# Rest tokens' second scores inside M's step, batch 0 by halves of its heads, and a new order, in a two-stage attention with an MLP on one core

## The chip, the cores and the metric

The kernel runs on one core of a Trainium2 chip. The metric is device time in microseconds for one execution. The core has five engines with queues of their own: TensorE (PE: matmuls; PEld is its weight load), VectorE (DVE), ScalarE (ACT), GpSimd (POOL, which here issues the loads) and SyncE (SP, which here issues the stores). An engine works its queue strictly in order; an instruction that waits for another engine holds up everything behind it in its own queue. Matmul results go to PSUM, eight banks of 128 partitions by 512 float32 numbers, from which VectorE or ScalarE read them.

## The reference

For each of 8 batches and 8 heads, with 576 tokens of 64 numbers, a pack of 32 queries `p` first attends over the tokens; then the 576 queries `q` attend over the 32 packed rows; the heads side by side go through an MLP with a squared relu:

```python
p_packed = sm_attn(p, k, v)          # 32 x 64 per head
out = sm_attn(q, p_packed, p_packed) # 576 x 64 per head
x = out, heads side by side          # 4608 x 512
h = relu(x @ w_in); y = (h * h) @ w_out   # 512 -> 2048 -> 512
```

`sm_attn` is softmax attention with scale 1/8 and the row's maximum taken off. Inputs and output are float32; the kernel multiplies in bfloat16.

## The kernel before, in words

Heads are handled in two groups of four (`qd` 0 and 1). For one batch the steps are, with their names in the planner and their lines:

- **T** (Tk, Tq; L440, L437): VectorE transposes of k and q after the loads.
- **S1** (L449/L451 in `s1`, L464 in `s1_both`): first scores, 32 pack rows for four heads by 576 tokens per group. `s1` makes one group with 128x128 matmuls; `s1_both` makes both groups with 64x32 tiles of the array that work side by side. Batch 0 (`SOLO`) uses `s1`, the others `s1_both`. Then max (L472), exponential with its sum (L476) and normalisation (L482, L483).
- **E** (L489): five 128x128 transposes per group into one PSUM bank, 4 or 5, and a copy to SBUF (`s1_out`).
- **PV, XT** (L504, L516): the packed rows; `extract` copies them out of the bank as `ppT`, `spread` reorders them with four small matmuls into the same bank, and `pq_block` writes them as blocks on a diagonal into `pq_bd` (four copies).
- **M** (L536): packed rows times w_in, 64x32 tiles, in four chunks of 512 columns; so the second attention's value product and w_in become one matrix. Chunks are copied out by `m_out` (two banks at once) or `m_half` (one bank).
- **S2** (L556, L567 in batch 0): second scores, tokens on partitions, 512 of the 576 tokens. **S2 rest** (L574, `s2_rest`): the last 64 tokens, four matmuls with 128x64 tiles into bank 4 or 5. Then max (L586), subtract (L591), exponential (L597), sum and reciprocal (L603, L604), product (L609).
- **N** (L618, L620): transposes of these weights into bank 4 or 5, N.b.0 for the first 256 tokens, N.b.1 for the rest, and copies to `a2`.
- **F1** (L633; L646 in batch 0, called FA and F1): M times weights, 16 blocks of 128 rows, into a pair of banks; relu (L655, L671) and square (L662, L664, L681) give `gT`.
- **F2** (L689, and L706 for the last tile): 16 matmuls of 512 columns for each tile of 128 tokens, into bank 6 or 7 (two early tiles in banks 5 and 3), a copy (`f2_out`) and four stores.

Banks are named by tiles. `ps` holds two pair tiles, banks 0 and 1 and banks 2 and 3, each `[128, 2, 512]`; banks 4 to 7 are four tiles of one bank each, `pb4` to `pb7`. `bank(u)` gives one bank, `pair(u)` a pair tile. The framework adds the waits between engines from the tiles that the instructions read and write.

The order is written out ahead of time by a planner (`Plan`). It holds streams of steps, each with its dependencies, its PSUM banks and set durations (the number beside an engine's name), and issues what is ready by a priority. `TABLE` corrects priorities ("o") and the choice between VectorE and ScalarE ("l"). Where the planner sees TensorE idle before the first F2, it fills in matmuls on zeros (`keep_clock`, L345). POOL issues the loads; the string `ORDER` names them, and among the early ones `TABLE` decides which goes first.

Of the kernel before, what the change touches and what calls it, by code (L numbers as in the profile page):

```python
# [53 lines left out]
class Plan:  # L54
# [193 lines left out]
TABLE = {'o': {'P.0': -301.77, 'X.0': -1069.94, 'P.2': -238.95, 'X.1': -188.5, 'La0': -1231.77, 'La1': -809.34,  # L248
# [45 lines left out]


def kernel_impl(tc, q, k, v, p, w_in, w_out, out):
# [10 lines left out]
    NT = TOK // P  # L307
    NKQ, NV, NR = 15, 5, 6
    VX = JT // 2
    SOLO = (0,)  # L310
    TOKH = (2 * P, S - 2 * P)

    with ExitStack() as ctx:
# [23 lines left out]
        pq_bd = [consts.tile([P, 4 * P], BF16, name=f"pq_bd{i}") for i in range(2)]  # L337
# [9 lines left out]
        def half(n):  # L347
            return ps[n // 2][:, n % 2, :] if n < 4 else ps[n - 2][:]
# [14 lines left out]
        def setup():  # L363
            nc.vector.memset(zero, 0.0)  # L364
            nc.vector.memset(pT_bd[:, :2], 0.0)
            nc.vector.memset(v_b[0][:64, :, GM * D:], 0.0)
            nc.vector.memset(pq_bd[0], 0.0)
            nc.vector.memset(pq_bd[1], 0.0)
# [55 lines left out]
        class Att:  # L424
            def __init__(self, b, t):
                self.b, self.t = b, t
                self.pq = pq_bd[b % 2]
                self.ps1, self.psm, self.pst = {}, {}, {}
# [38 lines left out]
            def at(self, qd, h):  # L467
                return h ^ 2 if qd and self.b not in SOLO else h

# [25 lines left out]
            def pv(self, qd, u):  # L495
                if qd == 0:
                    self.ps_bank = bank(u)
                    self.ps_pp = self.ps_bank[:, :P]
# [20 lines left out]
            def pq_block(self, h, eng):  # L519
                c = slice(32 * h, 32 * h + 32)  # L520
                cast(eng, self.pq[c].rearrange("p (qd x c) -> p x qd c", qd=NQD, x=2)[:, :, :, c],
                     self.ps_pq[c].rearrange("p (x qd i) -> p x qd i", x=2, qd=NQD))

            def pq_of(self, qd, dh):
                return self.pq[:, (2 * qd + dh) * P:(2 * qd + dh + 1) * P]
# [33 lines left out]
            def s2_half(self, x, u):  # L559
                if x == 0:  # L560
                    self.ps2h = {}
# [7 lines left out]

            def s2_rest(self, u):  # L570
                self.ps2r = bank(u)[:, :P]
                for dh in range(2):
# [4 lines left out]
            def src2(self, x):  # L577
                s = self.ps2r if x == 2 else self.ps2h[x] if x < 2 else self.ps2[:].rearrange("p c n -> p (c n)")
                return s.rearrange("p (g i) -> p g i", i=32)
# [453 lines left out]
```

## Time and profile before

| | |
|---|---|
| median of three runs | 256.63 us (256.39 to 256.83) |
| profiled execution | 256.86 us, span 255.1 us |
| granted TensorE clock | 0.999 |
| TensorE busy | 246.8 us, 97% |
| VectorE, ScalarE busy | 172.9 us (68%), 168.3 us (66%) |
| F2 (L689) | 560 matmuls of 512 columns, 380 ns from start to end each, overlapping |
| F1 (L633) | 448 matmuls of 288 columns, 286 ns each, overlapping |

Matmuls overlap, so the pace is read from the distance of their starts in the timeline and not from their mean duration. The time of the profiled execution is 1.8 us above its span, which begins with the first instruction and ends with the last. Before 30 us batch 0 works through its chain, with filling matmuls between; from there TensorE goes through F1, F2 and the next batches' steps mixed. In a profile line, what stands in brackets is the idle time of the engine before the instruction and what ended it.

### The profile page before, as it was taken

Reading aid. Unit: us, or ns where it says so; the run is one execution under the profiler, and the core shown is the slowest. Engines: PE = TensorE matmul, PEld = TensorE weight load, DVE = VectorE, ACT = ScalarE, POOL = GpSimd, SP = SyncE. Lnnn points to the kernel's source line nnn. Section 1 sums busy time; section 2 is a strip of 40 time slices with the busy share of each in tenths; the row PEclk is TensorE's granted clock in tenths of the full one; section 3 lists DMA queues with packets and bytes.
Section 4 is the critical chain, followed back from the end, with each engine's and each line's share of the span. In section 5 each row is a group of like instructions: output and inputs, shape, how many; then the busy total and the mean of one; then the engine's idle time right before and its main releaser. Section 6 shows DMA issues by size and latency. Waiting matters only on the chain.

```text
span 255.1 us, 5879 instructions
## 1 busy us (share of the span) xinstructions
PE 246.8 (97%) x2348; PEld 139.9 (55%) x2348; DVE 172.9 (68%) x339; ACT 168.3 (66%) x289; POOL 43.0 (17%) x76
## 2 busy tenths in 40 slices
PE   7898999999999999999999999999999999999993
PEld 5574665365545665466454555467454565365452
DVE  6678767896886797576369369967768667546300
ACT  7436999779629488688676791599461685669301
POOL 8746444332424300000000000000000000000000
PEclk9999999999999999999999999999999999999999
DMA  6999999999999999510112202211111211111132
GB/s 113 189 201 208 202 204 201 214 245 230 205 224 226 237 219 159 129 45 0 44 44 62 63 3 70 56 41 42 38 51 41 54 31 36 49 51 31 48 93 68
DMA packets 26619, 28.50 MB, mean 112 GB/s; under 512 B 5472, under 2 KB 18016, under 8 KB 26592
## 3 DMA queue, kind: packets, MB, share of 16 engines
q0 software_dynamic: 18960, 18.55, 44.4%
q1 hardware_dynamic: 7008, 9.38, 13.4%
q8 instruction: 18, 0.29, 0.4%
q10 hardware_dynamic: 624, 0.20, 0.3%
q14 instruction: 9, 0.07, 0.1%
HBM read 37.22 MB, written 9.44 MB: 183 GB/s over the span
## 4 chain that ended last, share of the span: by engine, by line
PE 87%; ACT 4%; DMA 3%; DVE 2%; POOL 1%; issue 1%; DVEq 0%; POOLq 0%
PE pb L689 46%; PE ps L633 22%; DMA q_b<-in_q_dram 3%; PE ps L556 3%; PE pb L504 2%; PE ps L536 2%; PE ps L464 2%; PE ps L646 2%; PE pb L489 2%; PE pb L618 1%; PE ps L689 1%; PE pb L706 1%; PE pb L536 1%; ACT r L655 1%; ACT gT L662 1%; ACT pq_bd L359 1%
## 5 line engine op out<-in xcount | busy, mean ns | idle before, releaser
L689 PE MATMUL pb<-w_out_b,gT 128*128 128x512 bf16 x544 | 142.9, 380 | 0.0
L689 PEld LDWEIGHTS <-gT 128*128 128x128 bf16 x560 | 51.5, 97 | 56.2 <-issue 5.0
L671 ACT ACTIVATE r<-ps 128x576 bf16<-128x576 f32 x112 | 71.9, 651 | 15.7 <-PE ps L633 11.2
L633 PE MATMUL ps<-a,M 128*128 128x288 bf16 x448 | 72.2, 286 | 0.0
L681 DVE TENSOR_TENSOR gT<-r 128x576 bf16<-128x576 bf16 x112 | 50.6, 457 | 28.8 <-ACT r L671 27.8
L633 PEld LDWEIGHTS <-M 128*128 128x128 bf16 x448 | 43.2, 98 | 21.1 <-issue 1.3
L476 ACT ACTIVATE e1x<-ps,n 128x576 bf16<-128x576 f32 x16 | 11.8, 748 | 13.8 <-DVE n L472 13.0
L359 ACT CAST M<-ps 128x1024 bf16<-128x1024 f32 (+1 forms) x18 | 16.5, 916 | 6.0 <-PE ps L536 5.9
L361 DVE COPY o_sb<-pb 128x512 f32<-128x512 f32 (+1 forms) x20 | 13.2, 662 | 8.5 <-PE pb L706 4.5
L359 ACT COPY o_sb<-pb 128x512 f32<-128x512 f32 (+1 forms) x16 | 9.3, 579 | 14.0 <-PE pb L689 12.8
L597 ACT ACTIVATE e<-d 128x1152 bf16<-128x1152 f32 (+2 forms) x10 | 9.6, 970 | 12.8 <-DVE d L591 12.7
L472 DVE TENSOR_REDUCE n<-ps 128x1 f32<-128x576 f32 x16 | 11.6, 749 | 7.3 <-PE ps L464 7.1
L345 PE MATMUL pb<-zero 128*128 128x256 bf16 x92 | 14.3, 305 | 1.5 <-DVE zero L364 1.1
L359 ACT CAST M<-pb 128x512 bf16<-128x512 f32 x28 | 15.3, 601 | 0.0
L414 POOL DMA_DIRECT2D v_b<-in_v_dram x16 | 11.2, 702 | 13.3 <-DMA k_b<-in_k_dram 9.9
L437 DVE STREAM_TRANSPOSE qT<-q_b 128x576 f32<-128x576 f32 x16 | 11.8, 758 | 1.9 <-DMA q_b<-in_q_dram 1.9
L359 ACT COPY a<-pb 128x512 bf16<-128x512 bf16 (+1 forms) x9 | 5.4, 634 | 11.5 <-PE pb L618 10.9
L409 POOL DMA_DIRECT2D q_b<-in_q_dram x16 | 8.9, 560 | 22.6 <-DVE kT L440 10.5
L603 DVE TENSOR_REDUCE t<-e 128x36 f32<-128x1152 bf16 (+2 forms) x10 | 11.1, 1105 | 2.1 <-ACT e L597 2.0
L440 DVE STREAM_TRANSPOSE kT<-k_b 128x576 f32<-128x576 f32 x16 | 11.9, 762 | 0.8 <-DMA k_b<-in_k_dram 0.8
L345 PEld LDWEIGHTS <-zero 128*128 128x128 bf16 x92 | 9.3, 109 | 3.8 <-DVE zero L364 1.1
L609 DVE TENSOR_TENSOR n<-e,r 128x1152 bf16<-128x1152 bf16 (+2 forms) x10 | 11.1, 1111 | 0.2
(78 smaller groups left out, 237.2 us busy)
## 6 DMA issues: line engine op xcount, KB each, us to landing
out_dram<-o_sb SPq DMA_DIRECT2D x140, 64.0 KB, 1.7
k_b<-in_k_dram POOLq DMA_DIRECT2D x16, 288.0 KB, 12.0
q_b<-in_q_dram POOLq DMA_DIRECT2D x16, 288.0 KB, 11.6
v_b<-in_v_dram POOLq DMA_DIRECT2D x8, 320.0 KB, 11.9
v_b<-in_v_dram POOLq DMA_DIRECT2D x8, 256.0 KB, 11.8
w_in_b<-in_moe_w_in_dram POOLq DMA_DIRECT2D x8, 256.0 KB, 10.3
w_out_b<-in_moe_w_out_dram POOLq DMA_DIRECT2D x8, 256.0 KB, 10.5
p_b<-in_p_dram POOLq DMA_DIRECT2D x1, 192.0 KB, 10.8
```

The source lines that it names most:

```text
L345: nc.tensor.matmul(half(7)[:, :2 * P], lhsT=zero[:, :P], rhs=zero, start=True, stop=True)
L359: nc.scalar.copy(dst, src)
L361: eng.tensor_copy(dst, src)
L414: nc.gpsimd.dma_start(self.v[64 * i:64 * i + 64, :, :n * D], src[:, :, i * GM * D:(i * GM + n) * D])
L437: nc.vector.transpose(self.qT[:, qd].rearrange("p s x -> p (s x)").bitcast(F32), self.t.q[qd][:].bitcast(F32))
L440: nc.vector.transpose(kT[:, qd].rearrange("p s x -> p (s x)").bitcast(F32).rearrange("p (x a j2) -> p j2 x a", a=32, j2=2), self.t.k[qd][: ...
L472: nc.vector.tensor_reduce(self.n1[:, qd:qd + 1], self.ps1[qd], axis=AX.X, op=ALU.max, negate=True)
L476: nc.scalar.activation(e1x[:, qd], self.ps1[qd], ACT.Exp, bias=self.n1[:, qd:qd + 1], accum_out=self.d1[:, qd:qd + 1])
L633: nc.tensor.matmul(ps[:, c], lhsT=a.M[:, qd, fb * FB:(fb + 1) * FB], rhs=a.a2[:, qd, c * HALF:(c + 1) * HALF], start=(qd == 0), stop=(qd = ...
L671: nc.scalar.activation(dst, src, ACT.Relu)
L681: eng.tensor_tensor(out=Att.cols(gT[:, fb, o:o + S]), in0=r, in1=r, op=ALU.mult)
L689: nc.tensor.matmul(po[t], lhsT=gT[:, fb, n0:n0 + P], rhs=w_out_b[:, fb, :], start=(fb == 0), stop=(fb == NFB - 1))
```

## The change

The diff touches these places:

- `ps` gets a third pair tile for banks 4 and 5; only banks 6 and 7 stay single tiles.
- For batches 2 to 7 (`FUSE`), `s2_rest` makes the last tokens' scores with 16 matmuls in 64x32 tiles, the two halves of the array's rows into banks 4 and 5, and is issued in the same piece as the first half of M. Its max and subtract (`SR`) read both banks.
- Batch 1 makes S1 with `s1`, one group at a time; `s1_both` is used in batches 2 to 7 (`DUAL`).
- Batch 0 goes by groups of heads: PV, extraction, spread and blocks for one group (`pv_solo`, `extract_solo`, `spread_solo`, `block_solo`), then the first 256 tokens' second scores for that group (`s2_one` and the chain `one_max` to `one_mul`, on 256 columns).
- In `pq_bd` the second group's four heads stand in the order h^1, the order that M's rows have for that group; the two groups lie `PQ` = 320 columns apart.
- The first half of the last tile is stored by two queues, as the second half was.
- `TABLE` is new throughout, and with it the order on every engine and the order of loads.

```diff
-        ps = [psum.tile([P, 2, 512], F32, name=f"ps{i}") for i in range(2)]
-        ps += [psum.tile([P, 512], F32, name=f"pb{i}") for i in range(4, 8)]
+        ps = [psum.tile([P, 2, 512], F32, name=f"ps{i}") for i in range(3)]
+        ps += [psum.tile([P, 512], F32, name=f"pb{i}") for i in range(6, 8)]
...
-            return ps[n // 2][:, n % 2, :] if n < 4 else ps[n - 2][:]
+            return ps[n // 2][:, n % 2, :] if n < 6 else ps[n - 3][:]
...
-                return h ^ 2 if qd and self.b not in SOLO else h
+                return h ^ 2 if qd and self.b in DUAL else h
...
+            def pv_solo(self, qd, u):
+                t = self.pvb[qd] = bank(u)
+                self.ps_pp = t[:, :P]
+                self.pv(qd, None)
+
+            def extract_solo(self, qd, eng):
+                self.tile_of("ppT", small, [P, NQD, 2, NP], BF16)
+                cast(eng, self.ppT[:, qd].rearrange("p pr i -> p (pr i)"), self.pvb[qd][:, 64 * qd:64 * qd + 64])
...
+            def s2_one(self, qd, u):
+                t = self.ps2q[qd] = bank(u)
+                for tt in range(2):
+                    for dh in range(2):
+                        nc.tensor.matmul(t[:, tt * P:tt * P + P], lhsT=self.qT[:, qd, tt * P:(tt + 1) * P, dh],
+                                         rhs=self.pq_of(qd, dh), start=(dh == 0), stop=(dh == 1))
...
             def s2_rest(self, u):
+                if self.b in FUSE:
+                    self.ps2r = ps[2][:, :, :64]
+                    for e in range(2):
+                        r = slice(64 * e, 64 * e + 64)
+                        for dh in range(2):
+                            for o in range(4):
+                                c0 = 4 * P + o % 2 * 32
+                                nc.tensor.matmul(self.ps2r[32 * o:32 * o + 32, e], lhsT=self.qT[r, o // 2, c0:c0 + 32, dh],
+                                                 rhs=self.pq_of(o // 2, dh)[r, r], start=(dh == 0), stop=(dh == 1))
+                    return
...
+            def first():
+                T[b].s2_rest(U[f"S2.{b}.1"])
+                mm(0)
...
+            return [Step(f"S2.{b}.1", [NO], [f"XT.{b}"] + [f"Tq.{b}.{qd}" for qd in QDS] + [f"N.{b - 1}.{qd}" for qd in QDS], banks=[(4, 5)]),
+                    Step(f"M.{b}.0", [[[("PE", 0.58, first)]]], [f"S2.{b}.1"] + pre(0), banks=[(0, 1, 2, 3)], mode=2),
...
-            return ([one(qd) for qd in QDS] if b in SOLO else hold()) + [two(qd) for qd in QDS]
+            return (hold() if b in DUAL else [one(qd) for qd in QDS]) + [two(qd) for qd in QDS]
...
-            out = [[("SP", 0.9, lambda: store(t, sl, 0, 2, nc.sync))], [("ACT", 0.9, lambda: store(t, sl, 2, 4, nc.scalar))]] if h else [[
-                ("SP", 1.8, lambda: store(t, sl))]]
+            out = [[("SP", 0.9, lambda: store(t, sl, 0, 2, nc.sync))], [("ACT", 0.9, lambda: store(t, sl, 2, 4, nc.scalar))]]
```

More of the change, by code (lines that the diff above doesn't have):

```diff
@@ L310, in kernel_impl @@
     SOLO = (0,)
+    DUAL = range(2, 8)
+    FUSE = range(2, 8)
     TOKH = (2 * P, S - 2 * P)
@@ L336, in kernel_impl @@
         pT_bd = consts.tile([P, B, NQD, 2, P], BF16, name="pT_bd")
-        pq_bd = [consts.tile([P, 4 * P], BF16, name=f"pq_bd{i}") for i in range(2)]
+        pq_bd = [consts.tile([P, 6 * P], BF16, name=f"pq_bd{i}") for i in range(2)]
         perm = consts.tile([P, 2, 2, P], BF16, name="perm")
         gT = consts.tile([P, NFB, 2 * S], BF16, name="gT")
-        ps = [psum.tile([P, 2, 512], F32, name=f"ps{i}") for i in range(2)]
-        ps += [psum.tile([P, 512], F32, name=f"pb{i}") for i in range(4, 8)]
+        ps = [psum.tile([P, 2, 512], F32, name=f"ps{i}") for i in range(3)]
+        ps += [psum.tile([P, 512], F32, name=f"pb{i}") for i in range(6, 8)]
         def keep_clock(n):
@@ L495, in pv @@
             def pv(self, qd, u):
-                if qd == 0:
+                if qd == 0 and u:
                     self.ps_bank = bank(u)
@@ L520, in pq_block, with spread_solo, block_solo @@
                 c = slice(32 * h, 32 * h + 32)
-                cast(eng, self.pq[c].rearrange("p (qd x c) -> p x qd c", qd=NQD, x=2)[:, :, :, c],
+                s = PQ + (-32 if h % 2 else 32)
+                cast(eng, self.pq[c, 32 * h:32 * h + 2 * s].rearrange("p (qd y) -> p qd y", qd=NQD)[:, :, :2 * P]
+                     .rearrange("p qd (x c) -> p x qd c", x=2)[:, :, :, :NP],
                      self.ps_pq[c].rearrange("p (x qd i) -> p x qd i", x=2, qd=NQD))
+            def pv_solo(self, qd, u):
[5 more added lines that the diff above has]
+                cast(eng, self.ppT[:, qd].rearrange("p pr i -> p (pr i)"), self.pvb[qd][:, 64 * qd:64 * qd + 64])
+            def spread_solo(self, qd):
+                for x in range(2):
+                    for pr in range(2):
+                        nc.tensor.matmul(self.pvb[qd][:, P + x * NP:P + x * NP + NP], lhsT=perm[:, x, pr], rhs=self.ppT[:, qd, pr],
+                                         start=(pr == 0), stop=(pr == 1))
+            def block_solo(self, qd, h, eng):
+                c = slice(32 * h, 32 * h + 32)
+                c0 = 32 * (h ^ qd)
+                cast(eng, self.pq[c, qd * PQ:qd * PQ + 2 * P].rearrange("p (x c) -> p x c", x=2)[:, :, c0:c0 + NP],
+                     self.pvb[qd][c, P:P + 2 * NP].rearrange("p (x i) -> p x i", x=2))
             def pq_of(self, qd, dh):
-                return self.pq[:, (2 * qd + dh) * P:(2 * qd + dh + 1) * P]
+                return self.pq[:, qd * PQ + dh * P:qd * PQ + (dh + 1) * P]
             def m(self, c, u, j=0, qds=range(NQD)):
@@ new lines, in wide, with one_max, one_sub @@
+            def wide(self, t, qd):
+                return self.of(t, qd).unsqueeze(3).to_broadcast([P, 2, QH, NP])
+            def one_max(self, qd):
+                self.tile_of("m2", small, [P, 36], F32, bufs=2)
+                nc.vector.tensor_reduce(self.of(self.m2, qd), self.ps2q[qd][:, :2 * P].rearrange("p (t h i) -> p t h i", t=2, h=QH), axis=AX.X, op=ALU.max)
+            def one_sub(self, qd):
+                self.tile_of("d2", small, [P, 36, 32], F32, bufs=1)
+                nc.vector.tensor_tensor(out=self.of(self.d2, qd), in0=self.ps2q[qd][:, :2 * P].rearrange("p (t h i) -> p t h i", t=2, h=QH),
+                                        in1=self.wide(self.m2, qd), op=ALU.subtract)
@@ new lines, in one_exp, with one_sum @@
+            def one_exp(self, qd):
+                self.tile_of("e2", small, [P, 36, 32], BF16, bufs=1)
+                nc.scalar.activation(self.of(self.e2, qd), self.of(self.d2, qd), ACT.Exp, scale=0.125)
+            def one_sum(self, qd):
+                self.tile_of("t2", small, [P, 36], F32, bufs=2)
+                self.tile_of("r2", small, [P, 36], F32, bufs=2)
+                nc.vector.tensor_reduce(self.of(self.t2, qd), self.of(self.e2, qd), axis=AX.X, op=ALU.add)
+                nc.vector.reciprocal(self.of(self.r2, qd), self.of(self.t2, qd))
@@ L585, in s2_max @@
                 g0, g1 = self.GR[x]
-                nc.vector.tensor_reduce(self.m2[:, g0:g1], self.src2(x), axis=AX.X, op=ALU.max)
+                src = self.src2(x)
+                m = self.m2[:, g0:g1]
+                nc.vector.tensor_reduce(m if len(src.shape) == 3 else m.rearrange("p (e g) -> p e g", e=2), src, axis=AX.X, op=ALU.max)
             def s2_sub(self, x):
@@ L590, in s2_sub @@
                 g0, g1 = self.GR[x]
-                nc.vector.tensor_tensor(out=self.d2[:, g0:g1], in0=self.src2(x),
-                                        in1=self.m2[:, g0:g1].unsqueeze(2).to_broadcast([P, g1 - g0, 32]), op=ALU.subtract)
+                src, d, m = self.src2(x), self.d2[:, g0:g1], self.m2[:, g0:g1].unsqueeze(2).to_broadcast([P, g1 - g0, 32])
+                if len(src.shape) == 4:
+                    d, m = (y.rearrange("p (e g) i -> p e g i", e=2) for y in (d, m))
+                nc.vector.tensor_tensor(out=d, in0=src, in1=m, op=ALU.subtract)
             def s2_exp(self, x):
@@ L753, in tr_steps @@
             elif nm == "k":
-                old = [f"S1.{b - 1}.{i}" for i in (QDS if b - 1 in SOLO else [1])]
+                old = [f"S1.{b - 1}.{i}" for i in ([1] if b - 1 in DUAL else QDS)]
             else:
-                old = [("S2.0.0", "SB.0.1", "SC.0.2")[i] if b == 1 else f"S2.{b - 1}.{i}" for i in range(3 if b == 1 else 2)]
+                old = [("SA.0.0", "SA.0.1", "SB.0.1", "SC.0.2")[i] if b == 1 else (f"S2.{b - 1}.0", f"M.{b - 1}.0" if b - 1 in FUSE else f"S2.{b - 1}.1")[i] for i in range(4 if b == 1 else 2)]
             return [Step(f"T{nm}.{b}.{qd}", [[[("DVE", 0.7, lambda qd=qd: (T[b].tr_k if nm == "k" else T[b].tr_q)(qd))]]],
@@ L773, in hold @@
                 return [Step(n0, [[[("-", 0.0, lambda: None)]]], [f"Tk.{b}.{qd}" for qd in QDS] + after, banks=HB),
-                        Step(nm, [[[("PE", 0.56, lambda: T[b].s1_both([U[n0], U[nm]]))]]], [n0], banks=HB, mode=2)] + chain
+                        Step(nm, [[[("PE", 0.54, lambda: T[b].s1_both([U[n0], U[nm]]))]]], [n0], banks=HB, mode=2)] + chain
             def two(qd):
@@ L779, in two @@
                                  [[("DVE", 0.41, lambda: T[b].s1_out(qd, V)), ("ACT", 0.59, lambda: T[b].s1_out(qd, A))]]],
[L780 to L781 removed]
+                            [f"SX.{b}.{qd}" if b in DUAL else f"S1.{b}.{qd}"], banks=AB, free=[(1, None)])
+            return (hold() if b in DUAL else [one(qd) for qd in QDS]) + [two(qd) for qd in QDS]
         def pv_steps(b):
             nm = f"PV.{b}.0"
+            if b in SOLO:
+                res = []
+                for qd in QDS:
+                    n1 = f"PV.{b}.{qd}"
+                    res.append(Step(n1, [[[("PE", 0.33, lambda qd=qd, n1=n1: T[b].pv_solo(qd, U[n1]))]]],
+                                    [f"E.{b}.{qd}", f"Lv.{b}.0", f"Lv.{b}.1", "I"], (), [("vb", 0, f"Lv.{b}.0")] if qd else [], banks=AB + OB, mode=1))
+                    res.append(Step(f"XT.{b}.{qd}", [NO, [[("DVE", 0.15, lambda qd=qd: T[b].extract_solo(qd, V)),
+                                                           ("ACT", 0.12, lambda qd=qd: T[b].extract_solo(qd, A))]],
+                                                     [[("PE", 0.085, lambda qd=qd: T[b].spread_solo(qd))]],
+                                                     [[("DVE", 0.15, lambda h=h, qd=qd: T[b].block_solo(qd, h, V)),
+                                                       ("ACT", 0.15, lambda h=h, qd=qd: T[b].block_solo(qd, h, A))] for h in range(QH)]],
+                                    [n1], free=[(3, n1)]))
+                return res
             return [Step(nm, [[[("PE", 0.33, lambda: T[b].pv(0, U[nm]))]]],
@@ L824, in m_steps, with outs, mm @@
-            return res
+            def outs(c):
+                return ([[("ACT", 0.91, lambda: T[b].m_out(c, A)), ("DVE", 1.14, lambda: T[b].m_out(c, V))]]
+                        + [[("ACT", 0.49, lambda x=x: T[b].m_half(c + 1, x, A)), ("DVE", 0.6, lambda x=x: T[b].m_half(c + 1, x, V))] for x in QDS])
+            def mm(c):
+                T[b].m(c, U[f"M.{b}.{c}"], 0)
+                T[b].m(c + 1, U[f"M.{b}.{c}"], 2)
+            def first():
+                T[b].s2_rest(U[f"S2.{b}.1"])
+                mm(0)
@@ new lines, in pre @@
+            def pre(c):
+                return [f"LWI.{x}.{i}" for x in (c, c + 1) for i in range(2)] + ([f1n(b - 2, NFB - 1)] if b > 1 else [])
+            if b not in FUSE:
+                return [Step(f"M.{b}.{c}", [[[("PE", 0.48, lambda c=c: mm(c))]], outs(c)], [f"XT.{b}/1.0"] + pre(c),
+                             banks=[x + (4, 5) for x in HB], free=[(1, None)], mode=2) for c in (0, 2)]
+            return [Step(f"S2.{b}.1", [NO], [f"XT.{b}"] + [f"Tq.{b}.{qd}" for qd in QDS] + [f"N.{b - 1}.{qd}" for qd in QDS], banks=[(4, 5)]),
+                    Step(f"M.{b}.0", [[[("PE", 0.58, first)]]], [f"S2.{b}.1"] + pre(0), banks=[(0, 1, 2, 3)], mode=2),
+                    Step(f"MX.{b}.0", [NO, outs(0)], [f"M.{b}.0"], free=[(1, f"M.{b}.0")]),
+                    Step(f"M.{b}.2", [[[("PE", 0.48, lambda: mm(2))]], outs(2)], [f"XT.{b}/1.0"] + pre(2),
+                         banks=[x + (4, 5) for x in HB], free=[(1, None)], mode=2)]
@@ L834, in chain @@
+            nm = f"S2.{b}.0"
             def chain(x, w):
@@ L851, in s2_steps @@
             if b in SOLO:
-                hn = [f"S2.{b}.0", f"SB.{b}.1"]
-                hs = [Step(hn[x], [[[("PE", 0.45, lambda x=x: T[b].s2_half(x, U[hn[x]]))]]] + front(x, 512) + chain(x, 512),
-                           pre, banks=AB + OB, free=[(2, None)]) for x in range(2)]
+                hn = [f"SA.{b}.0", f"SA.{b}.1", f"SB.{b}.1"]
+                hs = [Step(hn[x], [[[("PE", 0.23, lambda x=x: T[b].s2_one(x, U[hn[x]]))]], [[("DVE", 0.34, lambda x=x: T[b].one_max(x))]],
+                                   [[("DVE", 0.34, lambda x=x: T[b].one_sub(x))]], [[("ACT", 0.34, lambda x=x: T[b].one_exp(x))]],
+                                   [[("DVE", 0.55, lambda x=x: T[b].one_sum(x))]], [[("DVE", 0.34, lambda x=x: T[b].one_mul(x))]]],
+                           [f"XT.{b}.{x}", f"Tq.{b}.{x}"], banks=AB + OB, free=[(2, None)]) for x in range(2)]
@@ L858, in s2_steps @@
             return [Step(nm, [a] + front(3, 1024), pre, banks=HB, free=[(2, None)]),
-                    Step(nr, [r] + front(2, 128), pre, banks=AB, free=[(2, None)], mode=1),
-                    Step(f"C.{b}", chain(4, 1152), [nm, nr])] + [nstep(x, [f"C.{b}"], AB) for x in range(2)]
+                    Step(f"SR.{b}", front(2, 128), [f"M.{b}.0"], free=[(1, f"S2.{b}.1")]) if b in FUSE else
+                    Step(f"S2.{b}.1", [[[("PE", 0.12, lambda: T[b].s2_rest(U[f"S2.{b}.1"]))]]] + front(2, 128), pre, banks=AB, free=[(2, None)], mode=1),
@@ L862, in fh_steps @@
+                    Step(f"C.{b}", chain(4, 1152), [nm, f"SR.{b}" if b in FUSE else f"S2.{b}.1"])] + [nstep(x, [f"C.{b}"], AB) for x in range(2)]
         def fh_steps(x):
```

53 lines of the change are left out of this document (23 added, 30 removed), and 93 rows, old and new, of the table TABLE.

## The prediction

> **What bounds the kernel now.** I read the page first (span, engines, clock, chain), then the waits of TensorE, then the timelines of TensorE and ScalarE, then the groups by shape.
>
> ```profile
> span 255.1 us, 5879 instructions
> ...
> PE 246.8 (97%) x2348; PEld 139.9 (55%) x2348; DVE 172.9 (68%) x339; ACT 168.3 (66%) x289; POOL 43.0 (17%) x76
> ...
> PE 87%; ACT 4%; DMA 3%; DVE 2%; POOL 1%; issue 1%; DVEq 0%; POOLq 0%
> ```
>
> TensorE is the bound, and the waits say how tightly. These are TensorE's own, longest first; the columns are the total in us, how often, and the longest:
>
> ```profile
> PE ps L449 <- DVE kT L440: 1.3, 2, 0.9
> PE pb L345 <- DVE zero L364: 1.1, 1, 1.1
> PE ps L536 <- ACT r L655: 0.5, 1, 0.5
> PE pb L345 <- DVE m L586: 0.4, 1, 0.4
> ```
>
> All of them lie before 30 us. The timeline of TensorE (start, us, line, shape, count, idle before) shows no idle time from 30 us to the last matmul at 251.0; a matmul of 512 columns starts every 0.216 us there. So three things can move the time: idle time in the first 50 us, matmul work that is added or removed, and any wait that appears after 30 us, which costs its full length.
>
> TensorE, three places:
>
> ```profile
> 10.58 0.45 PE L489 MATMUL pb<-ident,e1n 128*128 128x128 bf16 x5 [0.15 <-DVE e1n L483]
> ...
> 11.22 0.45 PE L489 MATMUL pb<-ident,e1n 128*128 128x128 bf16 x5
> 11.82 0.49 PE L504 MATMUL pb<-e,v_b 128*64 128x32 bf16 x20
> ...
> 12.56 0.49 PE L504 MATMUL pb<-e,v_b 128*64 128x32 bf16 x20
> ...
> 25.12 0.40 PE L536 MATMUL ps<-w_in_b,ppT 64*32 64x512 bf16 x4 [0.49 <-ACT r L655]
> ...
> 53.69 0.44 PE L489 MATMUL pb<-ident,e1n 128*128 128x128 bf16 x5
> 53.97 0.65 PE L633 MATMUL ps<-a,M 128*128 128x288 bf16 x4
> 54.46 0.44 PE L489 MATMUL pb<-ident,e1n 128*128 128x128 bf16 x5
> ```
>
> ScalarE beside them:
>
> ```profile
> 11.07 1.33 ACT L359 COPY e<-pb 128x640 bf16<-128x640 bf16 x2 [0.51 <-PE pb L489]
> 13.91 1.06 ACT L359 CAST pq_bd<-pb 32x128 bf16<-32x128 f32 x4 [1.51 <-PE pb L516]
> ...
> 23.46 0.60 ACT L655 ACTIVATE r<-ps 128x512 bf16<-128x512 f32 x1 [0.62 <-PE ps L646]
> ...
> 24.48 0.59 ACT L655 ACTIVATE r<-ps 128x512 bf16<-128x512 f32 x1
> ...
> 54.50 1.28 ACT L359 COPY e<-pb 128x640 bf16<-128x640 bf16 x2
> ```
>
> Two readings decide the forecast. At 54.46 the second half's transposes (bank 5) start while the copy of the first half's (bank 4) is still to start, at 54.50: `pb4` and `pb5` are two tiles and don't wait for each other. At 25.12 it is otherwise: M's matmuls write the second bank of the pair tile `ps`, and their last reader, the relu of 23.46, ended at 24.06; they start at 25.12, right after the relu of 24.48 (ends 25.07), which reads the *first* bank of that pair. In the list of instructions this matmul does wait for that relu. Inside a pair tile, an access to one bank waits for another engine's access to the other bank.
>
> **The change part by part.**
>
> *The pair tile of banks 4 and 5.* The change makes `ps[2]` one tile of what were `pb4` and `pb5`. The changed kernel's instruction list has the waits that follow: the transposes E.0.1 into bank 5 wait for ScalarE's copy out of bank 4, the copy of E.0.1 waits for the PV.0.0 matmuls in bank 4, the ppT copy of the first heads waits for PV.0.1, the second half's S2 matmuls wait for the first half's max, and so on to batch 7. I walked the queues of TensorE, VectorE and ScalarE in the new order with each instruction's duration from its row; the same walk over the old order puts the first matmul of batch 1's F1 at 53.1 to 53.5 (trace: 53.19) and finds no wait over 0.2 us after 30 us, as the trace has it.
>
> Batch 0. Hops: 0.2 us from a matmul's issue to ScalarE's start (10.86 to 11.07), 0.05 back (25.07 to 25.12). Copy of E.0.0 ends 11.07+0.72 = 11.79; E.0.1 transposes 11.84 (were 11.22); PV.0.0 0.28 later, 0.42 long with its turn; copy of E.0.1 12.84 to 13.56; PV.0.1 13.6 (was 12.56), to 14.0. The first ppT copy, which the head split meant to follow PV.0.0, starts 14.2; 0.22, spread 0.15, second ppT 14.8 to 15.05, spread, and the block copies start at 15.4. Five of these (0.25 each, from 1.06 for four) come ahead of the first S2 matmuls: 16.7 (was 15.03). Its max waits for all eight blocks: 17.8 to 18.2. The second heads' S2 waits for that max, then max, two subs, exp, and two sets of sum, reciprocal and product at 256 columns (0.42 as the 256-column copy, 0.2 for a reciprocal) with a 0.69 us max of the other tokens between: N.0.0's transposes at 22.4 (were 20.02). N.0.1 comes at 27.8 (was 26.00): 1.8 lost. From there to batch 1's F1, M chunks 2 and 3, F2 tiles in bank 5 and E.1 sit beside users of bank 4: TensorE waits 0.54, 0.31, 0.25, 0.50, 0.50 (the last two: F2 in bank 5 behind the max and the subtract of batch 1's rest) and five times about 0.2. Idle time up to batch 1's F1 grows by **4.8**.
>
> Body. E.2 keeps its order, five transposes, one F1 of 0.49, five transposes; but the copy of 54.50 now holds the second five: 54.50+0.72+0.05 = 55.2 against 54.46, 0.7. Batch 2's N.2.0 stands two F2 matmuls behind E.3.0: round trip 0.28+0.20+0.71+0.05 = 1.24, less 0.28+0.43 = 0.5; N.2.1 behind N.2.0's copy 0.4. In batches 5 and 6, E.0 waits for the copy of the previous N.1. ScalarE comes to it after N.0's copy and two exponentials: 0.48+2×0.87+0.70+0.25 of hops = 3.2, where nine F2 matmuls cover 1.94 and E.0's own input is there at 2.3, so 0.87 each. E.1, two F2 behind E.0, waits for E.0's copy, 0.5 each as above. One at batch 7, 0.2. Sum 0.7+0.5+0.4+2×1.37+0.2 = 4.5, and about 0.8 in waits under 0.15: **5.3**. Bounds: 2 if ScalarE and VectorE run a tenth faster than the rows (the walk's total is then +6.3), 7 if a tenth slower.
>
> *Rest tokens in M's step (batches 2 to 7).* Removed: four 128*64 matmuls, 0.235 to the next start (43.02 to 43.25), and the turn of 0.1 ahead. Added: 16 of 64*32, 64 columns, next to M of the same shape, no turn. Nearest row: S1's 16×512 + 16×64 columns start to next in 0.64 (50.06 to 50.70); M's 16×512 take 0.44 without turns; so 0.20. Per batch −0.14: **−0.85**. Ends: 0.1 (column time alone: −1.4) and 0.30 (PV's 0.0185 each: −0.2). Max and subtract keep 128 columns (0.28 each) and stay on VectorE.
>
> *Batch 1's S1 one half at a time.* 8 matmuls of 128*128: 2×(0.45+0.06) = 1.02 against 0.70 with its turns, and two turns fewer near M: **+0.15** (0 to 0.3). *Spread of batch 0:* eight for four, **+0.1**.
>
> *At nothing:* four-head column order (the same block copies, 0.25 to 0.29 each); wider memsets of `pq_bd` (VectorE is idle 0.81 behind them, for p); w_in chunks 2 and 3 loaded behind k1 and w_out 0 and 1: in the trace one load lands each 1.3 us, so they land by 30, just ahead of use at 31.5 to 36 (cover gone: 1 to 2); the last tile's first half stored over both queues: ScalarE issues 0.83 at 246.3, idle until 249.35. SP has two DMAs fewer there; its tail (six from 249.96) is unchanged.
>
> Sum: 4.8+5.3−0.85+0.15+0.1 = **+9.5** on the profiled run's 256.86 (span 255.1 and 1.8 around it): 266.4. That run lies 0.23 above the median of 256.63, so I expect 266.2.
>
> [...]
>
> **The rivals.**
> 1. *The waits bind in batch 0 and 1 only*; in the body copies come early enough. For it: 68% and 66% busy VectorE and ScalarE. Against: 54.46 before 54.50. 4.8−0.6: 261.1.
> 2. *Faster: the head halves shorten batch 0's chain because no wait crosses banks.* Then ppT follows PV.0.0 at 12.4, spread, four blocks, S2 at 14.1 in place of 15.03: −0.9, with −0.6 of work 255.1 to 255.4. It decides only if E.0.1's transposes start before 11.8. Against it stand the waits in the list, and 0.8 more VectorE time for the two 256-column sets, which could eat the gain (256.5, no change).
> 3. *Worse: the late copies also push ScalarE's relus.* An F1 and one F2 take 0.71 and a relu 0.65, so lost time is caught up at 0.06 a step. Eight round trips losing another 0.5: 270.4.
>
> **How the numbers follow.** Forecast 0.76 (263 to 269); rival 1 0.10; rival 2 0.08, of which 0.05 faster and 0.03 no change; rival 3 0.06. The range leaves out rivals 2 and 3 (0.14): 260 to 269.5. Faster by over 0.2% 0.05, within 0.2% (about what this measurement can tell from no change) 0.03, slower 0.92.
>
> **What would show it.** TensorE's waits gain rows "ps L495 <- ACT e", "ps L699 <- ACT" and "ps L770 <- DVE", some 10 us in all; E.0.1's transposes start near 11.84; N.0.0 near 22.4; batch 1's first 288-column matmul near 58; TensorE's busy time grows little while its span grows. Wrong if the second transposes of a batch start while the copy of the first runs, or if the extra time is in matmuls.

## The result, and the profile after

The changed kernel takes 269.01 us (median of 4 runs, 268.29 to 269.26), beside 256.73 us for the kernel before, measured along with it (256.39 to 257.16): a ratio of 1.0473, 95% interval 1.0447 to 1.0499. The forecast was 266.2 us with a range of 260 to 269.5 us. The sign, the mechanism and most of the size were right; some 2.4 to 2.7 us of the loss (experiment 3) came from something that the sum did not have.

The page of the changed kernel, its parts 1, 2 and 4 (span, busy times, the granted TensorE clock in 40 slices, the chain by engine):

```profile
span 267.1 us, 5985 instructions
...
PE 251.4 (94%) x2399; PEld 141.8 (53%) x2399; DVE 179.5 (67%) x352; ACT 165.2 (62%) x287; POOL 43.1 (16%) x76
...
PEclk9967999999999999999999999999999999999999
...
PE 84%; ACT 6%; DVE 5%; DMA 2%; issue 2%; POOL 0%; DVEq 0%; POOLq 0%
```

TensorE's share of the chain fell from 87% to 84% and ScalarE and VectorE gained 5 points: TensorE now waits for them. The third and fourth digits of the clock row (slices of 6.7 us) are new too, 6 and 7 in place of 9. TensorE's waits in the changed kernel (total us, times, longest):

```profile
PE ps L495 <- ACT e L365: 1.7, 4, 0.6
PE ps L495 <- DVE e1n L489: 1.5, 2, 0.8
...
PE ps L565 <- DVE M L367: 0.9, 1, 0.9
PE ps L601 <- DVE m L614: 0.8, 1, 0.8
PE ps L544 <- DVE ppT L367: 0.7, 2, 0.4
...
PE ps L770 <- DVE M L367: 0.5, 1, 0.5
PE ps L510 <- ACT e L365: 0.5, 1, 0.5
```

L495 are the transposes E (L489 before), L565 is M, L601 the new score group of four heads, L544 the new spread, L770 is F2 and L510 is PV. The name `ps` stands for all three pair tiles; in experiment 1, which keeps the order and splits the third one, these waiting matmuls write tiles named `pb`, so the waits shown lie on the third pair, banks 4 and 5. The timeline of TensorE in the changed kernel (start, us, count, idle before and what ended it):

```profile
10.69 0.45 PE L495 MATMUL ps<-ident,e1n 128*128 128x128 bf16 x5
...
11.92 0.44 PE L495 MATMUL ps<-ident,e1n 128*128 128x128 bf16 x5 [0.45 <-ACT e L365]
...
24.55 0.39 PE L699 MATMUL ps<-ident,n 128*128 128x128 bf16 x4
...
60.46 0.66 PE L714 MATMUL ps<-a,M 128*128 128x288 bf16 x4
60.96 0.44 PE L495 MATMUL ps<-ident,e1n 128*128 128x128 bf16 x5
61.24 0.65 PE L714 MATMUL ps<-a,M 128*128 128x288 bf16 x4
62.44 0.44 PE L495 MATMUL ps<-ident,e1n 128*128 128x128 bf16 x5 [0.55 <-ACT e L365]
...
150.76 0.44 PE L495 MATMUL ps<-ident,e1n 128*128 128x128 bf16 x5 [0.77 <-DVE e1n L489]
151.04 0.59 PE L770 MATMUL pb<-w_out_b,gT 128*128 128x512 bf16 x2
151.98 0.44 PE L495 MATMUL ps<-ident,e1n 128*128 128x128 bf16 x5 [0.35 <-ACT e L365]
```

ScalarE beside them:

```profile
61.70 0.69 ACT L365 COPY e<-ps 128x640 bf16<-128x640 bf16 x1
...
150.01 0.70 ACT L365 COPY a<-ps 128x640 bf16<-128x640 bf16 x1
```

In before, the second five transposes of batch 2 started before the copy of the first five did. Here they start at 62.44, after the copy out of the other bank of the tile has ended at 62.39 (61.70 plus 0.69). From the F1 at 61.24 it is 1.20 us where 0.49 had been: 0.71 us lost, and 0.7 was forecast. At 150.76 the row names the normalised `e1n`, but its first group was ready at 150.00; the copy of `a` out of the other bank ended at 150.71. Nine F2 matmuls from 147.88 would have ended at 149.82, so 0.94 us are lost there (forecast 0.87).

The part that was not forecast stands in the windows of the changed kernel. After the length come TensorE, weight loads, VectorE, ScalarE and GpSimd, each with its busy time and its instructions, then the clock:

```profile
14.00:15.00 1.00, 0.31 (x8) 0.26 (x5) 0.47 (x3) 0.00 (x0) 0.39 (x1) 1.00 1.23 203
15.00:16.00 1.00, 0.81 (x9) 0.58 (x9) 0.66 (x1) 0.65 (x4) 0.69 (x1) 0.94 1.25 207
16.00:17.00 1.00, 0.57 (x5) 0.53 (x5) 0.00 (x0) 0.37 (x2) 0.39 (x2) 0.50 1.21 193
...
19.00:20.00 1.00, 1.00 (x10) 0.47 (x8) 0.97 (x4) 0.26 (x1) 0.15 (x1) 0.50 1.12 211
...
22.00:23.00 1.00, 1.00 (x10) 0.75 (x7) 0.95 (x3) 0.59 (x1) 0.63 (x1) 0.64 1.24 206
```

The granted clock fell to 0.50 from 15.9 to 22.7 us (a window in which it stood at 0.50 for a part shows a value between). N.0.0 came at 24.55 (forecast 22.4) and batch 1's first 288-column matmul at 60.46 (before 53.19, forecast "near 58").

### The profile page after: what moved, and what is told of

The parts are those of the page before. It is cut to its first block, busy times and chain, and to the rows that moved or that the text cites. A ratio compares the mean times of both kernels' runs of the same rounds, so it can differ in the third digit from the quotient of the medians.

```text
span 267.1 us, 5985 instructions
## 1 busy us (share of the span) xinstructions
PE 251.4 (94%) x2399; PEld 141.8 (53%) x2399; DVE 179.5 (67%) x352; ACT 165.2 (62%) x287; POOL 43.1 (16%) x76
## 4 chain that ended last, share of the span: by engine, by line
PE 84%; ACT 6%; DVE 5%; DMA 2%; issue 2%; POOL 0%; DVEq 0%; POOLq 0%
PE pb L770 42%; PE ps L714 20%; PE ps L565 3%; PE pb L351 2%; PE ps L585 2%; DMA k_b<-in_k_dram 2%; PE ps L510 2%; PE ps L495 2%; ACT e L365 2%; PE ps L770 2%; PE ps L699 2%; PE ps L727 1%; PE ps L470 1%; PE pb L787 1%; DVE pq_bd L367 1%
## 5 line engine op out<-in xcount | busy, mean ns | idle before, releaser
L770 PE MATMUL pb<-w_out_b,gT 128*128 128x512 bf16 x544 | 141.1, 380 | 0.3
L770 PEld LDWEIGHTS <-gT 128*128 128x128 bf16 x560 | 51.8, 97 | 60.1 <-issue 7.1
L752 ACT ACTIVATE r<-ps 128x576 bf16<-128x576 f32 x112 | 71.1, 651 | 19.1 <-PE ps L714 15.5
L714 PE MATMUL ps<-a,M 128*128 128x288 bf16 x448 | 71.0, 286 | 0.2
L365 ACT CAST M<-ps 128x512 bf16<-128x512 f32 (+1 forms) x39 | 26.2, 724 | 14.0 <-PE ps L565 13.6
L367 DVE COPY o_sb<-pb 128x512 f32<-128x512 f32 (+1 forms) x21 | 14.0, 667 | 13.3 <-PE pb L787 6.7
L365 ACT COPY o_sb<-pb 128x512 f32<-128x512 f32 (+1 forms) x15 | 8.6, 573 | 23.0 <-PE pb L770 21.8
L482 ACT ACTIVATE e1x<-ps,n 128x576 bf16<-128x576 f32 x16 | 11.8, 743 | 9.9 <-DVE n L478 9.7
L351 PE MATMUL pb<-zero 128*128 128x256 bf16 x91 | 15.2, 325 | 1.1 <-DVE zero L370 1.1
L415 POOL DMA_DIRECT2D q_b<-in_q_dram x16 | 8.9, 561 | 31.8 <-DVE kT L446 20.1
L420 POOL DMA_DIRECT2D v_b<-in_v_dram x16 | 11.2, 699 | 12.9 <-DMA k_b<-in_k_dram 9.4
L565 PE MATMUL ps<-w_in_b,ppT 64*32 64x512 bf16 x256 | 12.4, 387 | 0.9 <-DVE M L367 0.9
L365 ACT COPY e<-ps 128x640 bf16<-128x640 bf16 x12 | 8.3, 693 | 7.3 <-PE ps L495 6.0
L443 DVE STREAM_TRANSPOSE qT<-q_b 128x576 f32<-128x576 f32 x16 | 11.9, 760 | 0.5 <-DMA q_b<-in_q_dram 0.5
L665 DVE TENSOR_REDUCE m<-ps 128x32 f32<-128x1024 f32 (+1 forms) x14 | 10.5, 752 | 2.0 <-PE ps L585 0.8
## 6 DMA issues: line engine op xcount, KB each, us to landing
k_b<-in_k_dram POOLq DMA_DIRECT2D x16, 288.0 KB, 11.8
v_b<-in_v_dram POOLq DMA_DIRECT2D x8, 256.0 KB, 11.2
```

The costliest lines, as they stand in the source:

```text
L351: nc.tensor.matmul(half(7)[:, :2 * P], lhsT=zero[:, :P], rhs=zero, start=True, stop=True)
L365: nc.scalar.copy(dst, src)
L367: eng.tensor_copy(dst, src)
L443: nc.vector.transpose(self.qT[:, qd].rearrange("p s x -> p (s x)").bitcast(F32), self.t.q[qd][:].bitcast(F32))
L482: nc.scalar.activation(e1x[:, qd], self.ps1[qd], ACT.Exp, bias=self.n1[:, qd:qd + 1], accum_out=self.d1[:, qd:qd + 1])
L565: nc.tensor.matmul(half(at[qd])[o:o + 32], lhsT=self.ppT[64 * e:64 * e + 64, qd, pr, :], rhs=w_in_b[64 * e:64 * e + 64, qd * 2 + pr, c * W ...
```

## The experiments

The theory after the result: the waits by tile cost about 10 us as forecast, and the clock's fall, which those waits bring about, costs about 2.4 us more. Each experiment's ratio is against runs of the kernel before made along with it (medians 256.98 us in experiments 1 to 4, 257.26 in 5 to 8). The rivals: the new order, the head halves or the small tiles cost the time themselves; or the slow clock is hidden behind VectorE, which is busy 0.95 of that stretch.

### 1. Banks 4 and 5 as two tiles again

```diff
-ps = [psum.tile([P, 2, 512], F32, name=f"ps{i}") for i in range(3)]
-ps += [psum.tile([P, 512], F32, name=f"pb{i}") for i in range(6, 8)]
+ps = [psum.tile([P, 2, 512], F32, name=f"ps{i}") for i in range(2)]
+ps += [psum.tile([P, 512], F32, name=f"pb{i}") for i in range(4, 8)]
...
-self.ps2r = ps[2][:, :, :64]
+self.ps2r = [half(4 + e)[:, :64] for e in range(2)]
...
+if x == 2 and self.b in FUSE:
+    for e in range(2):
+        nc.vector.tensor_reduce(self.m2[:, 32 + 2 * e:34 + 2 * e],
+                                self.ps2r[e].rearrange("p (g i) -> p g i", i=32), axis=AX.X, op=ALU.max)
+    return
```

> The changed kernel with banks 4 and 5 as two tiles again; the rest tokens' scores still go to both banks, and their max and their subtract become two instructions each, one per bank. Order, fills and everything else are as in the changed kernel. Theory (waits by the tile cause the loss): the second half's transposes of batch 0 start at 11.2 to 11.3 us again, TensorE's waits on ScalarE's e and VectorE's M after 30 us go, the granted clock stays 1.00 through 11 to 23 us, batch 1's first 288-column matmul is near 52.7, and the time is 255.8 to 257.8 (before: 256.7, after: 269.0). Rival (the new order, the head halves or the small tiles cost the time): 262 or more.

Measured: 255.84 us, 0.9958 of before (0.9937 to 0.9978). The subtract is split like the max, so VectorE has 12 instructions more; the order of TensorE's work is that of the changed kernel, fills included. The 12 us are gone, and the rest of the change is a small gain: this version beats both kernels. TensorE and ScalarE in it, batch 2:

```profile
53.88 0.44 PE L495 MATMUL pb<-ident,e1n 128*128 128x128 bf16 x5
54.16 0.65 PE L718 MATMUL ps<-a,M 128*128 128x288 bf16 x4
54.65 0.44 PE L495 MATMUL pb<-ident,e1n 128*128 128x128 bf16 x5
```

```profile
54.63 1.28 ACT L365 COPY e<-pb 128x640 bf16<-128x640 bf16 x2
```

The second transposes go into bank 5 at 54.65 while ScalarE copies out of bank 4 from 54.63: as in before. The clock row of the page:

```profile
PEclk9799999999999999999999999999999999999999
```

It shows 9 in the slices where the changed kernel had 6 and 7, and a 7 in the second slice: batch 0's k came late in this profile, TensorE waited 2.3 us for `kT`, and ahead of the first transposes its matmuls took longer (the two of 512 columns at 8.99 took 1.06 us, in the changed kernel's profile at 8.57 0.61; the 14 fills at 9.97 took 1.97, there at 9.08 1.69). So two expected marks are missed here. The second transposes stand at 12.48, not 11.2 to 11.3, and the first five at 11.78 (10.69 in the changed kernel's profile); the two are 0.70 apart, against 1.23 there and 0.64 in before. Batch 1's first 288-column matmul stands at 53.39, not near 52.7. Experiment 7's kernel differs from this one in its last store alone, and its profile has the clock at 9 throughout: there the two marks are 11.25 and 52.13.

From batch 1's first 288-column matmul to the last tile's first 256-column matmul, TensorE needs 190.67 us here (53.39 to 244.06) and 195.75 us in the changed kernel (60.46 to 256.21), in the same order: **the waits in the body cost 5.08 us** (forecast 5.3).

The transposes at 54.65 have no idle time ahead of them, though ScalarE reads the other bank from 54.63; at the same place the changed kernel has 0.55 us. The wait in the changed kernel is the program's own: it goes when the declaration is split.

### 2. The pair tile alone, in the kernel before

```diff
-ps = [psum.tile([P, 2, 512], F32, name=f"ps{i}") for i in range(2)]
-ps += [psum.tile([P, 512], F32, name=f"pb{i}") for i in range(4, 8)]
+ps = [psum.tile([P, 2, 512], F32, name=f"ps{i}") for i in range(3)]
+ps += [psum.tile([P, 512], F32, name=f"pb{i}") for i in range(6, 8)]
```

> The kernel before with one edit: banks 4 and 5 are one tile of two banks, in the order of before, nothing else of the change. Theory: 264 to 267, by a walk of its queues with the rows' durations +8.5 us, of which 2.8 lie ahead of batch 1's first 288-column matmul (near 56, before 53.2) and 5.5 to 6 in waits after it. Rival (the loss is in the new order): within 2 us of before, 255 to 258.5.

Measured: 265.03 us, 1.0312 of before (1.0286 to 1.0337), so +8.0 us. Batch 1's first 288-column matmul is at 56.21 (near 56 expected), +3.0 us; the body takes 196.25 us in place of 190.72, +5.5 us. The old order loses at the same kind of place (TensorE):

```profile
11.80 0.44 PE L489 MATMUL ps<-ident,e1n 128*128 128x128 bf16 x5 [0.45 <-ACT e L359]
...
58.26 0.44 PE L489 MATMUL ps<-ident,e1n 128*128 128x128 bf16 x5 [0.61 <-ACT e L359]
```

Two edits of one declaration, in two orders, so go the same way: with the tile merged +8.0 us, with it split −13 us. The new order is not to blame.

### 3. More fills: the clock held up

```diff
 def s1_tr(self, qd, u):
+    if self.b in SOLO and qd: keep_clock(4)
 def pv_solo(self, qd, u):
+    if qd: keep_clock(4)
 def spread_solo(self, qd):
+    keep_clock(3)
 def s2_one(self, qd, u):
+    keep_clock(5 + qd)
```

> The changed kernel with 25 more fill matmuls (0.109 us each) where TensorE waits between 11 and 18 us: 4 ahead of the second transposes, 4 ahead of the second PV, 3 ahead of each spread, 5 and 6 ahead of the two score groups of batch 0. Theory (the fall of the granted clock at 16 to 23 us costs 2.4 us that the sum did not have): the granted clock stays at 1.00 there, N.0.0's transposes start near 22.5 in place of 24.55, batch 1's first 288-column matmul near 58 in place of 60.4, and the time is 266.0 to 267.4. Rival (the stretch is bound by VectorE and ScalarE, and a slow TensorE is hidden): 268.5 to 269.5. Second rival (the extra fills themselves delay the work): over 269.5.

Measured: 266.64 us, 1.0367 of before (1.0338 to 1.0396). With 25 more matmuls on the engine that bounds the kernel, the changed kernel is 2.4 us faster. Windows and timeline of TensorE:

```profile
16.00:17.00 1.00, 0.95 (x12) 0.73 (x10) 0.00 (x0) 0.51 (x4) 0.56 (x1) 1.00 1.22 208
...
19.00:20.00 1.00, 1.00 (x14) 0.56 (x10) 1.00 (x3) 0.75 (x2) 0.60 (x2) 1.00 1.12 214
```

```profile
22.24 0.39 PE L705 MATMUL ps<-ident,n 128*128 128x128 bf16 x4
...
58.15 0.67 PE L720 MATMUL ps<-a,M 128*128 128x288 bf16 x4
```

The clock stays at 1.00, N.0.0 is at 22.24 and batch 1's F1 at 58.15. The clock's fall cost 2.4 us by the times (2.7 by the two ratios), and what is left is the forecast: 58.15 − 53.19 = 4.96 us in the head (forecast 4.8), and 266.64 − 256.98 = 9.66 us in all (forecast 9.5). The rival that hides the slow clock behind VectorE falls.

### 4. Fewer fills: what held N.0.0

```diff
-if e == "PE" and p.start < end:
+if e == "PE" and p.start < end and p.step.name not in ("N.0.0", "N.0.1"):
     self.keep(self.fills(p.start - free.get(e, 0.0), p.start))
```

> The changed kernel without the 20 fill matmuls that the planner put ahead of N.0.0 and the 10 ahead of N.0.1. Theory (in the changed kernel those 20, two of them at half speed, stand in TensorE's queue when the products are already there, since what came before them was late): N.0.0 starts at 22.7 to 23.0 in place of 24.55 though the clock still falls at 16 us, and the time is 266.6 to 267.8. Rival (N.0.0 waits for its products or for bank 4, and the fills only fill that wait): N.0.0 stays at 24.3 to 24.6 and the time at 268.7 to 269.3.

Measured: 268.03 us, 1.0427 of before (1.0403 to 1.0451): 1.0 us faster than the changed kernel, less than the expected 266.6 to 267.8. TensorE, and its windows:

```profile
22.39 0.59 PE L699 MATMUL ps<-ident,n 128*128 128x128 bf16 x4 [0.69 <-ACT M L365]
...
25.48 2.81 PE L727 MATMUL ps<-a,M 128*128 128x256 bf16 x16
```

```profile
20.00:21.00 1.00, 1.00 (x6) 0.49 (x4) 0.93 (x4) 0.07 (x1) 0.89 (x2) 0.50 1.14 200
...
26.00:27.00 1.00, 1.00 (x7) 0.69 (x6) 0.76 (x4) 0.84 (x3) 0.27 (x2) 0.50 1.23 203
```

For comparison, VectorE's last product for N.0.0 and TensorE's fills in the changed kernel:

```profile
22.25 0.42 DVE L633 TENSOR_TENSOR n<-e,r 128x256 bf16<-128x256 bf16 x1
```

```profile
22.05 2.67 PE L351 MATMUL pb<-zero 128*128 128x256 bf16 x20
```

Counted from the first transposes of batch 0, N.0.0 starts after 11.9 us in place of 13.9. In the changed kernel its products were there at 22.67 and it came at 24.55, so those 20 fills, begun late at 22.05 and partly at half speed (2.67 us, 2.36 in experiment 1), did stand in its way. (In experiment 3 the products were there at 22.15 and N.0.0 came at 22.24.) But without them the clock stays at 0.50 until 27.3, the 16 matmuls of F1 take 2.81 us in place of 2.22, and half of the gain is lost again. The theory's place was right and its size wrong: with the fills the clock was back at 22.7, without them at 27.3.

### 5. The price of the small tiles

Experiment 1's kernel with the four 128*64 matmuls of before in the place of the 16 small ones (L644 the 16, L649 the four):

```diff
 def s2_rest(self, u):
     self.ps2r = bank(u)[:, :P]
-    if self.b in FUSE:
+    if False:
```

With the branch off (in the max and the subtract too), the four matmuls behind it run, into bank 4, and one max and one subtract read them.

> The kernel of the first experiment (banks 4 and 5 as two tiles, 255.8 us) with one edit: in the same place of the same order, batches 2 to 7 compute the rest tokens' scores with the four 128*64 matmuls of the kernel before, into bank 4, with one max and one subtract. It prices the 16 small matmuls. Theory (from the trace of after: the 16 small ones take about 0.08 us ahead of M and need no turn, the four took 0.235 and two turns of 0.1 here): 6 x 0.25 to 0.35 us slower than the first experiment, 257.2 to 258.0. By the prediction's value of 0.20 for the 16, it would be 6 x 0.14 to 0.24, 256.6 to 257.3. Rival (TensorE has slack there, or the added VectorE instructions eat it): 255.5 to 256.2.

Measured: 256.93 us, 0.9990 of before (0.9971 to 1.0009) where experiment 1 had 0.9958: some 0.8 us slower, though the two intervals overlap a little. In the trace, TensorE with the four, and then with the 16 in the changed kernel, with M alone behind:

```profile
101.41 0.30 PE L649 MATMUL pb<-pq_bd,qT 128*64 128x128 bf16 x4
101.64 0.63 PE L565 MATMUL ps<-w_in_b,ppT 64*32 64x512 bf16 x16
102.20 2.33 PE L774 MATMUL pb<-w_out_b,gT 128*128 128x512 bf16 x10
```

```profile
110.77 0.26 PE L644 MATMUL ps<-pq_bd,qT 64*32 64x64 bf16 x13
...
111.40 2.33 PE L770 MATMUL pb<-w_out_b,gT 128*128 128x512 bf16 x10
113.66 0.62 PE L565 MATMUL ps<-w_in_b,ppT 64*32 64x512 bf16 x16
114.22 1.04 PE L770 MATMUL pb<-w_out_b,gT 128*128 128x512 bf16 x4
```

(Of the 16, three records lie between M's own.) M alone takes 0.56 us from start to next start, with the four ahead of it 0.79, with the 16 ahead 0.63. So the four cost 0.23, the 16 cost 0.07, and the change saves 0.16 us per batch, 0.97 us over the body (191.64 against 190.67). My expectation for this run priced extra turns for the four and was too high; the prediction's 0.14 per batch was near.

### 6. Batch 1's first scores by both halves

```diff
-DUAL = range(2, 8)
+DUAL = range(1, 8)
```

> The kernel of the first experiment with batch 1's first scores by both halves in 64*32 tiles again, as in the kernel before (the order changes only around 26 to 40 us). The prediction priced one half at a time at +0.15 us (0 to 0.3). Theory: 255.5 to 256.0, that is 0 to 0.3 us faster than the first experiment. Rival (one half at a time lets batch 1's chain start earlier): 256.3 or more.

Measured: 266.15 us, 1.0335 of before (1.0309 to 1.0361), 10 us slower than experiment 1, which neither theory expected. The edit changes the kinds of steps, and with the old priorities the planner made another order: the first 288-column matmul is at 62.08 and follows new waits, among them

```profile
PE ps L565 <- ACT e1x L482: 1.9, 1, 1.9
...
PE pb L495 <- ACT M L365: 0.8, 1, 0.8
PE ps L470 <- ACT o_sb L365: 0.7, 1, 0.7
```

and the granted clock fell to 0.50 from 54.5 to 64.8 us (0.63 in the window from 54 to 56, 0.81 in that from 64 to 66). So this run doesn't price the step. It shows how closely the priorities fit one set of steps: with one step of another kind, the order that the planner makes of batches 1 and 2 loses 10 us.

### 7. The last tile's first store on one queue

```diff
-out = [[("SP", 0.9, lambda: store(t, sl, 0, 2, nc.sync))], [("ACT", 0.9, lambda: store(t, sl, 2, 4, nc.scalar))]]
+out = [[("SP", 0.9, lambda: store(t, sl, 0, 2, nc.sync))], [("ACT", 0.9, lambda: store(t, sl, 2, 4, nc.scalar))]] if h else [[
+    ("SP", 1.8, lambda: store(t, sl))]]
```

> The kernel of the first experiment with the store of the last tile's first half on SyncE's queue alone, as in the kernel before. The prediction priced the second queue at nothing. Theory: within 0.3 us of the first experiment, 255.5 to 256.2. Rival (SyncE's queue of six stores sets the end): 0.4 to 1 us slower.

Measured: 255.92 us, 0.9948 of before (0.9930 to 0.9967), against 0.9958 for experiment 1: no difference. Pricing this part at nothing was right.

### 8. No fills where nothing else waits

Experiment 1's kernel with experiment 4's edit.

> The kernel of the first experiment without the 20 fills ahead of N.0.0 and the 10 ahead of N.0.1, so TensorE is idle some 2.1 and 0.9 us there, with no waits between banks 4 and 5. Theory (idle stretches of TensorE pull the granted clock down): the clock falls to about 0.5 within some us after 18 to 20 us, the matmuls of 21 to 25 us take twice their time, and the time is 256.5 to 258. Rival (an idle stretch of 2 us does not pull it down, the fills are not needed): 255.4 to 256.0 and a clock of 1.00 throughout.

Measured: 256.86 us, 0.9984 of before (0.9960 to 1.0008), 0.7 us slower than experiment 1 by the two ratios, whose intervals overlap; the clock decides. TensorE's wait, and its windows:

```profile
PE pb L703 <- DVE n L633: 2.2, 1, 2.2
```

```profile
20.00:21.00 1.00, 0.00 (x0) 0.00 (x0) 0.93 (x4) 0.40 (x1) 0.39 (x1) 1.00 1.15 203
...
23.00:24.00 1.00, 1.00 (x9) 0.51 (x8) 0.97 (x4) 0.89 (x2) 0.68 (x1) 0.77 1.25 206
24.00:25.00 1.00, 1.00 (x7) 0.69 (x6) 0.96 (x4) 0.95 (x3) 0.50 (x1) 0.50 1.24 205
```

An idle stretch from 19.8 to 21.9 that costs nothing by itself (the products are not there earlier) is followed by a half clock from 23.5 to 26.9, when TensorE is fully busy again. In this profile the theory holds, but the fall is not certain. This profile's k was late as in experiment 1, with a first stretch at half clock that ended at 13.28 us (its 14 fills at 9.86 took 3.17 us, in the changed kernel 1.69), and it is the longest of the ten runs; only the shape of the clock is read from it. By the clock of the whole execution the ten runs line up: the one at 1.000 took 255.90 us, the five at 0.991 to 0.993 took 256.21 to 256.98, and the four at 0.984 to 0.987 took 257.45 to 258.80. A late k can have a part in the last four.

## Why the prediction was right, and where its size was off

**What bounds the kernel.** Right: TensorE bounds it, and idle time counts in full. The 5.08 us that the body lost are waits of TensorE, and they went when the tile was split.

**The pair tile: the mechanism.** Right, shown from both sides (experiments 1 and 2).

**Head, +4.8 us.** The changed kernel lost 7.27 us up to batch 1's F1 (60.46 − 53.19). With the clock held up it is 4.96, and the marks fall where the prediction's walk put them: second transposes 11.80 (11.84 forecast), N.0.0 22.24 (22.4), N.0.1 27.84 (27.8), F1 58.15 ("near 58"). The walk was right.

**The missing term.** The step of the sum that fell short is the head's: it took each matmul's duration from a trace in which the clock stood at 1.00 (the "rows"), and counted idle time of TensorE as lost time only. Idle time has a second price here. The waits left TensorE busy 0.54, 0.31, 0.81 and 0.57 us of each us from 13 to 17, and the clock was at 0.50 from 15.9 to 22.7. That alone cost 2.4 us (experiment 3). It showed at N.0.0, which counted from the first transposes lies 2.2 us later than in experiment 3. The products were 0.4 us late, and 1.8 came through the fills, whose number is fixed when the program is built: 20 of them stood ahead of N.0.0, late and slow, when there was little left to fill (experiment 4).

**Body, +5.3 us.** 5.08 measured. Batch 2's second transposes lost 0.71 (0.7 forecast), batch 5's E.0 0.94 (0.87) and E.1 0.51 (0.5: 1.22 from 150.76 to 151.98, less 0.28 and 2×0.216). The other waits stand where the walk had them: batch 2's N.2.0 and N.2.1 at 89.50 and 90.55 (idle 0.35 and 0.24), and batch 6's E.0 and E.1 at 179.82 and 181.04 with the same idle times as batch 5's, 0.77 and 0.35.

**Rest tokens, −0.85 us.** 0.97 measured. Both sizes were too large, the four matmuls at 0.335 (0.23 measured) and the 16 at 0.20 (0.07), and the errors cancelled; that the term came out near is luck. The 0.97 is the price against the four in the new order. Against before, experiment 1's kernel gains 1.1 us in all (0.9958), and no run here divides that between head and body.

**Batch 1's S1, +0.15 us.** Not settled; experiment 6 changed more than this step. **Last store, nothing.** Right (experiment 7). The column order, the memsets and the order of the loads were not tried on their own.

**The rivals.** Rival 1 (waits in the head alone, 261.1) falls with the 5.08 in the body. Rival 3 (late copies push the relus, 270.4) falls too: the body lost less than forecast. Rival 2's time, 255.1 to 255.4, or 256.5 if the added VectorE work eats the gain, was near what the change gives once no wait crosses the banks: 255.84, and in experiment 7's profile the first S2 matmuls stand at 14.11, where it had 14.1. Its condition, second transposes before 11.8, failed in the changed kernel (11.92).

**The signs.** The wait rows came as named; those of 0.2 us and more on `ps`, kT's left out, make 8.5 us (some 10 forecast). "TensorE's busy time grows little" was wrong: 246.8 to 251.4 us, so of the two signs against the forecast the second, extra time in matmuls, came in part. In experiment 7's profile, with as many matmuls (2399) and the clock at 9 throughout, it is 247.0. Of the 4.4 us between, the half clock can have brought some 2.8, an estimate: half of the 5.54 us for which the changed kernel's TensorE was busy from 15.88 to 22.72. Where the rest comes from was not shown.

## What to carry to other kernels

In this program a tile is the unit of waiting: merging two buffers that different engines use in turn makes neighbours wait for each other, even where the order, the data and the banks stay the same. If one instruction is to read both buffers at once, count what all the other users of them pay; here six maxima and six subtracts were saved at the price of 13 us (experiment 1 against the changed kernel). And where the granted clock falls after waits, as it did here (0.50 from 15.9 to 22.7 us, at 2.4 us by experiment 3), price idle time in a dense head twice, once for the wait and once for the slow work after it, and don't trust a fixed number of filler matmuls to fit once the work in front of them has moved.

## What the runs showed of the hardware

The half clock came in stretches of 3.4 us or of two or three times that. In the changed kernel, windows of 0.05 us show the clock at 1.00 up to 15.85, at 0.50 from 15.90 to 22.70 and at 1.00 again from 22.75. By the shares of the windows at their edges the stretches lasted from 15.88 to 22.72 us in the changed kernel (6.84), from 17.1 to 27.34 in experiment 4 (10.24), from 54.52 to 64.76 in experiment 6 (10.24) and from 23.54 to 26.94 in experiment 8 (3.40). The first one there ended at 13.28, and by the durations of its fills it began near 9.9 (3.4).

Ahead of three of these falls TensorE had waits but was not idle throughout: in the last 3.4 us at 1.00 it was busy 2.16 us (changed kernel, 12.5 to 15.9), 1.91 us (experiment 4, 13.6 to 17.0) and 1.57 us (experiment 8, 20.1 to 23.5). But the busy time does not decide it alone: in the changed kernel TensorE was busy only 1.91 us from 5.64 to 9.05, and there the clock stayed at 1.00. What else counts, these runs do not settle.
